# A third buffer for raw weights, a reordered opening, and constant products on TensorE ahead of the dense stage

## The chip, the cores and the metric

The kernel runs on one core of a Trainium2 chip. A core has five engines that run side by side and wait for each other by semaphores: TensorE (PE; its weight loads are listed as PEld), VectorE (DVE), ScalarE (ACT), GpSimd (POOL) and SyncE (SP), which here issues the DMA transfers from main memory. The metric is the device time of one execution in microseconds; the time before is 622.99 us, the median of three runs (621.7 to 623.39).

## The reference

Three stages follow each other.

```
# 1 attention-like scan, per batch and head (4 x 8), 768 tokens, head size 32, state 16
y = (C B^T * decay(i,j), causal) @ x  +  C @ state * decay_to_i
state = decay_full * state + sum_j decay_from_j * B_j x_j
x = y as 3072 tokens x 256
# 2 dense stage, w_a and w_b 256 x 1536, w_out 1536 x 256
x = ((x @ w_a) * (x @ w_b)) @ w_out
# 3 routed stage, 8 experts: each token goes to the expert of its largest logit
e = argmax(x @ w_gate); out = p[e] * sigmoid(x @ w_output_gate)[e] * relu(x @ w1[e]) @ w2[e]
```

The weights w_a, w_b, w_out come as 64-bit floats.

## The kernel before

**Tiling.** The 3072 tokens are 24 chunks of 128 tokens (index t), six to a batch. The dense stage takes them in nine blocks, BLK = 2, 2, 2, 2, 4, 4, 4, 2, 2 chunks. Its 1536 inner columns are 12 slices (index f) of 128. A unit (m, f) is block m times slice f: `unit_a` and `unit_b` make the two products on TensorE, VectorE multiplies them (L540), ACT and POOL split the result into two parts `gh` and `gl` (L427, L428), and `unit_o` adds it into the output. Each product is three TensorE passes over high and low parts (`mm3`, L513), so a unit of 256 tokens is 18 matmuls.

**Weights.** `load_w(f)` (L434) brings one slice of the three weights into a buffer `raw` by three DMAs (L439 twice, L442). `split_w(f)` turns the 64-bit numbers into a high part `whi` and a low part `wlo` in six pieces: ACT makes `u` (L464), VectorE does `low3` (L468), `sign` (L472) and `join` (L476), ACT rounds to `whi` (L480), VectorE subtracts to `wlo` (L483). The pool `stg` holds the raw slices; it has two buffers (L72), so the load of slice f+2 waits until slice f has been read.

**A chunk of the scan.** `tr` transposes B and C on TensorE (L339) and ACT copies them out, scaled (`cd`, L343, and `BT`, L345). `cb` multiplies them (L365, `pcb`), and VectorE multiplies the result with the decay mask `lm` that POOL has made (L303): this is the mask product (L369, `mt`). `ys` makes the outputs and the new state's part on TensorE (L386 to L396, `py`); ACT and VectorE split the output into `xh` (L402) and `xl` (L403), and VectorE updates the state (L407, L411). `prep` makes the scaled B and C for two chunks on POOL (`cp`, `Cq`, `Bq`, L295) and the masks.

**Decays.** `decays(r)` works out the decay factors of half r of the batches on VectorE, some 30 small instructions (L213 to L252), transposes them (`ex`, L207) and reduces the chunk totals (`tot` on POOL, L257, `tots` on VectorE, L264).

**What sets the order.** Each engine works its instructions off in the order in which they stand. From L993 the first steps are written out by hand (the opening). Behind them the units run in phases; after each product `tick` takes some steps of the scan from a list, two background steps (`bgstep`) and, by a rate, some pieces of the weight split from the list `dq` (`dstep`). Within that a scheduler places instructions of the four compute engines. A unit that needs a slice that is not yet split first takes the pieces that are missing. In the first three phases run blocks 0 to 3 with slices 0 to 5 while chunks 2 to 8 of the scan are worked; later phases run the other slices and blocks.

Of the kernel before, what the change touches and what calls it, by code (L numbers as in the profile page):

```python
# [7 lines left out]
F32 = mybir.dt.float32  # L8
# [10 lines left out]
def kernel(  # L19
# [52 lines left out]
    stg = ctx.enter_context(tc.tile_pool(name="stg", bufs=2))  # L72
# [93 lines left out]
    def load_bc(u):  # L166

        v = wk.tile([P, 2, G, H, N], F32, tag="BCin", name="BCin")
        for j, src in ((1, B), (0, C)):
            for i in range(G):  # L170
                b, c = divmod(u * G + i, NCH)
                nc.sync.dma_start(
                    out=v[:, j, i], in_=src[b, :, c * P:(c + 1) * P, :].rearrange("h p n -> p h n"))
        BCin[u] = v
# [12 lines left out]
    rfs = cst.tile([NR, 2, P], F32, name="rfs")  # L187
# [5 lines left out]
    def decays(r):  # L193
# [5 lines left out]
        ar = araw[:, r, :]  # L199
        rf, rs = rfs[:, 0], rfs[:, 1]  # L200
        a0, T, A, Eb, t2, t3 = (small(n) for n in ("a0", "T", "A", "Eb", "t2", "t3"))
        bc = lambda t, n=SUB: t.unsqueeze(2).to_broadcast([NR, n, SP_])
# [37 lines left out]

        def ends():

            q = st["q"]
            V.tensor_copy(out=A, in_=a0)
            for i in range(SUB - 1):
                V.tensor_scalar(out=A[:, i + 1:], in0=A[:, i + 1:], scalar1=T[:, i:i + 1], scalar2=None, op0=ALU.mult)
            for i in range(1, SUB):
                V.tensor_scalar(out=Eb[:, 0:i], in0=Eb[:, 0:i], scalar1=T[:, i:i + 1], scalar2=None, op0=ALU.mult)
            V.tensor_tensor(out=sub(q[:, 1]), in0=sub(q[:, 0]), in1=bc(A), op=ALU.mult)
            V.tensor_tensor(out=sub(q[:, 2]), in0=sub(rs), in1=bc(Eb), op=ALU.mult)  # L250
            V.tensor_tensor(out=t3[:, 0:1], in0=T[:, 0:1], in1=Eb[:, 0:1], op=ALU.mult)
            V.tensor_copy(out=q[:, 3], in_=t3[:, 0:1].to_broadcast([NR, P]))  # L252
# [14 lines left out]
        return dict(new=new, factors=factors, pairs=pairs, ends=ends, tot=tot, tots=tots,  # L267
# [55 lines left out]
    def attn_stages(t):  # L323
# [51 lines left out]
        def ys(alt=False):  # L375
# [23 lines left out]
            if m not in xT:  # L399
# [3 lines left out]
            nc.vector.tensor_tensor(out=lo[:, :, i0:i0 + P], in0=py,  # L403
                                    in1=hi[:, :, i0:i0 + P].bitcast(F32), op=ALU.subtract)
            if c < NCH - 1:
# [4 lines left out]
                if c > 0:  # L410
                    nc.vector.scalar_tensor_tensor(out=Sst, in0=Sst, scalar=dec[:, t:t + 1], in1=tm,  # L411
                                                   op0=ALU.mult, op1=ALU.add)

# [31 lines left out]
    def split_w(f):  # L445
# [7 lines left out]
        def wide_pieces(s):  # L453
# [1058 lines left out]
```

## Time and profile before

| | us |
|---|---|
| median of three runs | 622.99 |
| the profiled execution | 621.96 |
| its span, first to last instruction | 620.3 |
| TensorE busy | 569.3 (92%) |
| VectorE busy | 325.5 (52%) |
| ScalarE busy | 243.8 (39%) |
| GpSimd busy | 248.4 (40%) |

The profile is of one execution. Busy time is the sum of an engine's instructions without its waits. Of the 51 us in which TensorE is idle, 23.9 lie in the first 50 us and 8.3 in the next 50; from 100 to 400 us it is idle for 1.2 us. The granted clock is that of TensorE; 1.00 stands for 2.4 GHz and 0.50 for 1.2 GHz. Until the record's first change, at 43.5 us, the row shows 1.00 whatever the clock was; matmuls of 256 columns start 0.21 us apart at 21 us and 0.12 us apart at 51 us, which is the ratio of the two levels.

### The profile page before, as it was taken

The numbers are of one execution on the slowest core, as the hardware profiler recorded it, in microseconds if no ns is written. First come the engines' busy times: TensorE is split into PE (matmuls) and PEld (weight loads), VectorE is DVE, ScalarE is ACT, GpSimd is POOL, SyncE is SP. The second block draws the span as 40 slices with busy tenths as digits, with TensorE's granted clock in tenths as the row PEclk, the third lists the DMA queues.
The fourth block names the chain that finished last, engine by engine and source line by source line (L and its number), as shares of the span: only waits on it lengthen the run. The fifth ranks groups of instructions, "written<-read, shape, count | busy, mean of one in ns | idle before, by whom it ended". The sixth has DMA issues, their size and how long they took to land. (4 is left out here: it accounts for less than half of the span.)

```text
span 620.3 us, 11180 instructions
## 1 busy us (share of the span) xinstructions
PE 569.3 (92%) x4188; PEld 496.4 (80%) x4188; DVE 325.5 (52%) x894; ACT 243.8 (39%) x533; POOL 248.4 (40%) x319
## 2 busy tenths in 40 slices
PE   4369987999999999999999999999899999999991
PEld 2247867999897777777777889899788999999991
DVE  6779986224744434344232334544857556847620
ACT  3335553344333332332342233353345435445530
POOL 5547664333634433434222322364334433333111
PEclk9998997999999999999999999999999999999996
DMA  8597450002213210211000001221528345245000
GB/s 154 133 143 173 125 131 1 1 1 35 45 29 52 26 28 1 35 42 12 1 1 18 19 0 38 70 87 28 167 74 275 109 143 173 83 138 183 24 22 20
DMA packets 104920, 44.09 MB, mean 71 GB/s; under 512 B 81982, under 2 KB 99592, under 8 KB 104864
## 3 DMA queue, kind: packets, MB, share of 16 engines
q1 hardware_dynamic: 102128, 36.24, 23.7%
q0 software_dynamic: 2736, 7.12, 3.7%
q8 instruction: 34, 0.56, 0.4%
q14 instruction: 22, 0.18, 0.1%
HBM read 36.85 MB, written 6.95 MB: 71 GB/s over the span
## 5 line engine op out<-in xcount | busy, mean ns | idle before, releaser
L513 PE MATMUL pb<-xh,whi 128*128 128x256 f32 (+1 forms) x216 | 73.2, 339 | 1.7 <-ACT as__4671 L530 0.9
L513 PE MATMUL pa<-xh,whi 128*128 128x256 f32 (+1 forms) x216 | 72.0, 333 | 0.5 <-ACT xh L402 0.5
L513 PE MATMUL px<-gh,whi 128*128 128x256 f32 (+1 forms) x216 | 70.9, 328 | 0.0
L513 PE MATMUL pa<-xl,whi 128*128 128x256 f32 (+1 forms) x216 | 69.8, 323 | 0.0
L513 PE MATMUL px<-gl,whi 128*128 128x256 f32 (+1 forms) x216 | 69.2, 321 | 0.6 <-POOL gl L428 0.6
L513 PE MATMUL pa<-xh,wlo 128*128 128x256 f32 (+1 forms) x216 | 69.5, 322 | 0.0
L513 PE MATMUL px<-gh,wlo 128*128 128x256 f32 (+1 forms) x216 | 69.3, 321 | 0.0
L513 PE MATMUL pb<-xl,whi 128*128 128x256 f32 (+1 forms) x216 | 69.2, 320 | 0.0
L513 PE MATMUL pb<-xh,wlo 128*128 128x256 f32 (+1 forms) x216 | 69.1, 320 | 0.0
L1101 ACT ACTIVATE hh<-ph 128x384 fp32r<-128x384 f32 (+3 forms) x64 | 34.0, 531 | 69.7 <-PE ph L513 57.1
L1102 DVE SCALAR_TENSOR_TENSOR hl<-ph,hh 128x384 fp32r<-128x384 f32 (+3 forms) x64 | 38.7, 605 | 39.3 <-ACT hh L1101 33.8
L303 POOL TENSOR_SCALAR_AFFINE_SELECT lm<-EX 128x256 f32<-128x256 f32 x96 | 48.5, 541 | 24.2 <-DVE mt L369 22.6
L1121 PE MATMUL py<-eh,hh 128*128 128x256 f32 x200 | 57.0, 285 | 0.4 <-DVE hl L1102 0.4
L1121 PE MATMUL py<-el,hh 128*128 128x256 f32 x200 | 56.2, 281 | 0.0
L1121 PE MATMUL py<-eh,hl 128*128 128x256 f32 x200 | 56.1, 280 | 0.0
L1137 POOL DMA_INDIRECT out_dram<-yo,si x28 | 29.8, 1064 | 54.5 <-ACT yo L1134 47.7
L646 POOL DMA_INDIRECT xg<-x2d,gi x28 | 29.8, 1063 | 52.8 <-ACT lgx L661 36.9
L513 PEld LDWEIGHTS pb<-xh,whi 128*128 128x128 f32 x216 | 41.2, 191 | 10.7 <-issue 4.4
L513 PEld LDWEIGHTS pa<-xh,whi 128*128 128x128 f32 x216 | 41.3, 191 | 7.8 <-issue 3.7
L513 PEld LDWEIGHTS px<-gh,whi 128*128 128x128 f32 x216 | 41.0, 190 | 5.3 <-issue 2.1
L513 PEld LDWEIGHTS pa<-xh,wlo 128*128 128x128 f32 x216 | 41.4, 192 | 3.6 <-issue 0.3
L513 PEld LDWEIGHTS pa<-xl,whi 128*128 128x128 f32 x216 | 41.4, 192 | 3.3 <-issue 0.4
(685 smaller groups left out, 1402.3 us busy)
## 6 DMA issues: line engine op xcount, KB each, us to landing
raw<-in_moe_w_dram SPq DMA_DIRECT2D x30, 512.0 KB, 3.5
x2d<-xr SPq DMA_DIRECT2D x12, 272.0 KB, 2.2
xin<-in_x_dram SPq DMA_DIRECT2D x24, 128.0 KB, 2.9
raw<-in_moe_w_a_dram SPq DMA_DIRECT2D x12, 256.0 KB
raw<-in_moe_w_b_dram SPq DMA_DIRECT2D x12, 256.0 KB, 3.6
raw<-in_moe_w_out_dram SPq DMA_DIRECT2D x12, 256.0 KB, 4.1
BCin<-in_B_dram SPq DMA_DIRECT2D x26, 64.0 KB, 3.2
BCin<-in_C_dram SPq DMA_DIRECT2D x26, 64.0 KB, 3.1
```

Of the source, the lines that this page charges most:

```text
L303: nc.gpsimd.affine_select(out=Lm[t][:, :, s * SP_:(s + 1) * SP_], in_=exq(4 + s, b, c0 + i, 1).to_broadcast([P, H, SP_]), pattern=[[0, H], ...
L513: nc.tensor.matmul(out=out_, lhsT=l_, rhs=r_, start=first and i == 0, stop=last and i == 2, skip_group_check=skip)
L646: nc.gpsimd.indirect_dma_start(out=xg[:, q, :], out_offset=None, in_=x2d[0:nr, :], in_offset=bass.IndirectOffsetOnAxis(ap=sel["gi", i][:, ...
L1101: nc.scalar.activation(out=hh, in_=ph, func=AF.Relu)
L1102: V.scalar_tensor_tensor(out=hl, in0=ph, scalar=0.0, in1=hh.bitcast(F32), op0=ALU.max, op1=ALU.subtract)
L1121: nc.tensor.matmul(out=po, lhsT=l_[:, s_], rhs=r_, start=(f == 0 and j == 0 and q % 2 == 0), stop=(f == NF2 - 1 and j == 2), skip_group_ch ...
L1137: ins = nc.gpsimd.indirect_dma_start(out=out, out_offset=bass.IndirectOffsetOnAxis(ap=si[0:n_], axis=0), in_=yo, in_offset=None, bounds_ch ...
```

## The change

The pool of raw slices gets a third buffer. The loads of the first chunks are issued one chunk at a time, x of chunk 1 and all of chunk 0 and 1's B and C ahead of any weights; slices 0, 1 and 2 are loaded in the opening; later loads are taken from the list `dq` (`more_w`). The split of slice 1 moves from the opening into `dq`; pieces of slice 0's second and third part move ahead of steps of the scan. Eight small steps of `decays(0)` go to POOL (`parts`). `decays(1)` is put in the list at chunk 9 instead of 7, and its pieces stand ahead of `prep` there. The state update goes ahead of `xl` (L403). The function `warm` puts 15 products of a constant with itself on TensorE; nothing reads them. The tiles `u` share the buffers of `xr` and `x2T` for slices under 6, and from slice 6 on have one buffer instead of two. `rfs` moves into a shared buffer.

```
-    stg = ctx.enter_context(tc.tile_pool(name="stg", bufs=2))
+    stg = ctx.enter_context(tc.tile_pool(name="stg", bufs=3))
...
+        def parts(g=None):
+            g = g or V
+            g.tensor_copy(out=A, in_=a0)
+            for i in range(SUB - 1):
+                g.tensor_scalar(out=A[:, i + 1:], in0=A[:, i + 1:], scalar1=T[:, i:i + 1], scalar2=None, op0=ALU.mult)
+            for i in range(1, SUB):
+                g.tensor_scalar(out=Eb[:, 0:i], in0=Eb[:, 0:i], scalar1=T[:, i:i + 1], scalar2=None, op0=ALU.mult)
+            g.tensor_tensor(out=all_, in0=T[:, 0:1], in1=Eb[:, 0:1], op=ALU.mult)
...
-                    tl["u"] = wk.tile([P, 3 * DM], U32, tag="w64v", name="u", bufs=2)
+                    tag = ("xr", "x2T")[f % 2] if f < NE else "w64v"
+                    tl["u"] = wk.tile([P, 3 * DM], U32, tag=tag, name="u", bufs=1)
...
         load_a(0)
-        load_bc(0)
+        load_bc(0, 0)
         consts_early()
         load_x(0)
+        load_bc(0, 1)
+        load_x(1)
         load_w(0)
-        load_x(1)
-        load_bc(1)
         load_w(1)
+        load_bc(1, 0)
         load_x(2)
+        load_bc(1, 1)
         load_x(3)
+        load_w(2)
         load_a(1)
...
-                if t == 7:
-                    d1 = decays(1)
-                    nop = lambda: None
-                    bg.extend([d1["new"], d1["factors"], d1["pairs"], d1["ends"], nop, nop, nop, nop,
-                               d1["ex"](0, 4), d1["ex"](4, 4), d1["tot"], d1["tots"]])
+                if t == 9:
+                    d1 = decays(1)
+                    bg.extend(d1[k_] for k_ in ("new", "factors", "pairs", "parts", "ends"))
...
+        def warm(n):
+            t_ = pp([P, P], name="warm")
+            for _ in range(n):
+                nc.tensor.matmul(out=t_, lhsT=ones, rhs=ones, start=True, stop=True)
...
         s0["tr"]()
+        warm(2)
+        dc["parts"](nc.gpsimd)
         dc["ex"](4, 2)()
...
         s1["tr"]()
+        warm(3)
...
         dc["tot"]()
+        wb[0]()
+        wb[1]()
+        wb[2]()
+        wb[3]()
         s1["cb"]()
+        warm(2)
         s0["ys"](True)
+        warm(3)
         wa[5]()
+        wb[4]()
+        wb[5]()
+        wo[0]()
         dc["tots"]()
-        wb[0]()
         s1["ys"]()
-        for f_ in wb[1:] + wo:
+        warm(3)
+        for f_ in wo[1:]:
             f_()
```

**Where instructions stand.** On SP, the load of slice 2 before (what is in square brackets is what the instruction waits for; DMAHW is an earlier DMA, the others are engines):

```order
L439 DMA raw<-in_moe_w_a_dram 128x2x256 [waits DMAHW6_49]
L439 DMA raw<-in_moe_w_b_dram 128x2x256 [waits DMAHW7_49]
L442 DMA raw<-in_moe_w_out_dram 128x512 [waits DMAHW0_49]
L179 DMA xin<-in_x_dram 128x8x32 [waits DMAHW1_49]
L179 DMA xin<-in_x_dram 128x8x32 [waits DMAHW2_49]
L191 DMA araw<-in_a_dram 96x128 [waits DMAHW3_49]
```
```order
L179 DMA xin<-in_x_dram 128x8x32 [waits DMAHW0_49]
L179 DMA xin<-in_x_dram 128x8x32 [waits DMAHW1_49]
L439 DMA raw<-in_moe_w_a_dram 128x2x256 [waits DMAHW2_49,DVE_49,Activation_49]
L439 DMA raw<-in_moe_w_b_dram 128x2x256 [waits DMAHW3_49]
L442 DMA raw<-in_moe_w_out_dram 128x512 [waits DMAHW4_49]
```

The first piece ends with the loads of slice 1, the second is that of slice 2. In the changed kernel slice 1 and slice 2 stand on SP as follows:

```order
L442 DMA raw<-in_moe_w_a_dram 128x2x256 [waits DMAHW2_49]
L442 DMA raw<-in_moe_w_b_dram 128x2x256 [waits DMAHW3_49]
L445 DMA raw<-in_moe_w_out_dram 128x512 [waits DMAHW4_49]
L172 DMA BCin<-in_B_dram 128x8x16 [waits DMAHW5_49]
L172 DMA BCin<-in_C_dram 128x8x16 [waits DMAHW6_49]
L178 DMA xin<-in_x_dram 128x8x32 [waits DMAHW7_49]
L172 DMA BCin<-in_B_dram 128x8x16 [waits DMAHW0_49]
L172 DMA BCin<-in_C_dram 128x8x16 [waits DMAHW1_49]
L178 DMA xin<-in_x_dram 128x8x32 [waits DMAHW2_49]
L442 DMA raw<-in_moe_w_a_dram 128x2x256 [waits DMAHW3_49]
L442 DMA raw<-in_moe_w_b_dram 128x2x256 [waits DMAHW4_49]
L445 DMA raw<-in_moe_w_out_dram 128x512 [waits DMAHW5_49]
```

The load of slice 2 no longer waits for VectorE and ACT, and stands ahead of the second half of `a` and of x of chunks 4 and 5.

On ACT, from the output of chunk 1 (`xh<-py`) to the copies `cd` and `BT` of chunk 2, before:

```order
L402 ACTIVATE xh<-py 128x2x128
L480 ACTIVATE whi<-t 128x256
L464 ACTIVATE u<-raw 128x256
L480 ACTIVATE whi<-t 128x256
L464 ACTIVATE u<-raw 128x768
L480 ACTIVATE whi<-t 128x768
L464 ACTIVATE u<-raw 128x768
L530 ACTIVATE as__362<-pa 128x256
L464 ACTIVATE u<-raw 128x768
L343 ACTIVATE cd<-ptr,head_81 128x128 x2
L345 ACTIVATE BT<-ptr 128x256
```

and in the changed kernel:

```order
L405 ACTIVATE xh<-py 128x2x128
L484 ACTIVATE whi<-t 128x256
L468 ACTIVATE u<-raw 128x768 x2
L534 ACTIVATE as__372<-pa 128x256
L346 ACTIVATE cd<-ptr,head_81 128x128 x2
L348 ACTIVATE BT<-ptr 128x256
L484 ACTIVATE whi<-t 128x768
```

Between them stood two pieces of slice 0, slice 1 whole and the `u` of slices 2 and 3; now one piece of slice 0 and the `u` of slices 1 and 2.

On VectorE, a part of `decays(1)` before, between the multiplications L540 of the units of the third phase's first half:

```order
L238 TENSOR_SCALAR q_1054<-rfs,t_981 96x32
L246 TENSOR_SCALAR A_978<-A_978,T_977 96x3
L540 TENSOR_TENSOR as__905<-pb,as__905 128x256
L246 TENSOR_SCALAR A_978<-A_978,T_977 96x2
L248 TENSOR_SCALAR Eb_979<-Eb_979,T_977 96x1
L246 TENSOR_SCALAR A_978<-A_978,T_977 96x1
L248 TENSOR_SCALAR Eb_979<-Eb_979,T_977 96x2
L249 TENSOR_TENSOR q_1054<-q_1054,A_978 96x128
L248 TENSOR_SCALAR Eb_979<-Eb_979,T_977 96x3
L476 SCALAR_TENSOR_TENSOR t<-u,t 128x768
```

and its first instructions in the changed kernel (`as__1136` there is the multiplication that is called `as__1170` before):

```order
L544 TENSOR_TENSOR as__1136<-pb,as__1136 128x256
L476 SCALAR_TENSOR_TENSOR t<-raw 128x768
L487 TENSOR_TENSOR wlo<-t,whi 128x768
L544 TENSOR_TENSOR as__1175<-pb,as__1175 128x256
L480 SCALAR_TENSOR_TENSOR t<-u,t 128x768
L588 COPY x2T<-px_878 128x256
L213 MEMSET q_1848 96x96
L213 MEMSET q_1848 96x64
L544 TENSOR_TENSOR as__1203<-pb,as__1203 128x256
L487 TENSOR_TENSOR wlo<-t,whi 128x768
L213 MEMSET q_1848 96x32
L214 MEMSET Eb_1822 96x4
```

All of `decays(1)` on VectorE has moved behind the multiplication `as__1136`; its `tots` follows later still, ahead of the state update of chunk 9.

## Rows read from the trace of the kernel before

**Rows 1.** Windows: length, then busy (count) of PE, PEld, DVE, ACT, POOL, clock, DMA share, GB/s

```profile
36.06:99.10 63.04, 52.76 (x465) 43.24 (x465) 53.76 (x138) 30.67 (x71) 42.14 (x54) 0.91 0.58 131
104.53:200.00 95.47, 94.83 (x872) 87.73 (x871) 39.78 (x120) 38.23 (x101) 40.24 (x64) 1.00 0.16 24
...
43.50:50.20 6.70, 6.67 (x48) 4.83 (x49) 3.74 (x10) 2.18 (x5) 4.34 (x7) 0.50 0.72 212
...
94.30:101.35 7.05, 5.16 (x22) 4.54 (x23) 5.94 (x13) 1.26 (x2) 3.47 (x6) 0.53 0.00 0
```

**Rows 2.** Timeline of TensorE: start, length, what, [idle before it <- what ended it]

```profile
17.64 0.80 PE L386 MATMUL py<-BT,Sst 64*128 64x128 f32 x4 [1.73 <-DVE Sst L407]
...
20.38 0.58 PE L513 MATMUL pa<-xh,whi 128*128 128x256 f32 x1 [0.50 <-ACT xh L402]
...
34.48 1.24 PE L365 MATMUL pcb<-cd,BT 32*128 32x256 f32 x8 [11.56 <-ACT BT L345]
...
87.74 0.82 PE L207 MATMUL pd<-ident,q 96*128 96x96 f32 x8
...
96.19 1.22 PE L365 MATMUL pcb<-cd,BT 32*128 32x256 f32 x4 [3.84 <-DVE stm L407]
```

**Rows 3.** Timeline of ACT between the first two outputs and chunk 2

```profile
19.94 0.38 ACT L402 ACTIVATE xh<-py 128x256 fp32r<-128x256 f32 x1 [3.25 <-PE py L396]
23.03 0.42 ACT L480 ACTIVATE whi<-t 128x256 fp32r<-128x256 f32 x1 [2.71 <-DVE t L476]
...
30.18 0.37 ACT L530 ACTIVATE as__362<-pa 128x256 f32<-128x256 f32 x1
32.72 0.91 ACT L464 ACTIVATE u<-raw 128x768 f32<-128x768 f32 x1 [2.17 <-DMA raw<-in_moe_w_out_dram]
33.55 0.60 ACT L343 ACTIVATE cd<-ptr,head 128x128 f32<-128x128 f32 x2
34.04 0.38 ACT L345 ACTIVATE BT<-ptr 128x256 f32<-128x256 f32 x1
```

**Rows 4.** Timeline of SP, issues of the raw slices and of x

```profile
4.08 0.58 SPq L179 DMA_DIRECT2D xin<-in_x_dram  x1
...
24.65 0.37 SPq L439 DMA_DIRECT2D raw<-in_moe_w_a_dram  x1
```

**Rows 5.** VectorE by line, 36.06 to 99.10: count | busy, mean ns | idle before

```profile
L369 DVE TENSOR_TENSOR mt<-pcb,lm 128x256 f32<-128x256 f32 (+1 forms) x21 | 9.6, 503 | 3.9 <-PE pcb L365 3.9
L483 DVE TENSOR_TENSOR wlo<-t,whi 128x768 fp32r<-128x768 f32 x8 | 8.7, 1091 | 0.1
L472 DVE SCALAR_TENSOR_TENSOR t<-raw 128x768 uint32<-128x768 uint32 x7 | 8.5, 1217 | 0.0
L476 DVE SCALAR_TENSOR_TENSOR t<-u,t 128x768 uint32<-128x768 uint32 x8 | 8.5, 1057 | 0.0
L468 DVE TENSOR_SCALAR raw<-raw 128x768 uint32<-128x768 uint32 x7 | 4.6, 651 | 0.0
```

**Rows 6.** Timeline of VectorE

```profile
2.75 0.22 DVE L218 TENSOR_SCALAR araw<-araw 96x128 f32<-96x128 f32 x1 [1.31 <-DMA araw<-in_a_dram]
...
9.18 0.45 DVE L252 COPY q<-t 96x128 f32<-96x128 f32 x1
...
36.06 1.35 DVE L369 TENSOR_TENSOR mt<-pcb,lm 128x256 f32<-128x256 f32 x3
...
94.13 0.32 DVE L264 TENSOR_REDUCE dec<-dtmp 128x12 f32<-128x96 f32 x1 [2.94 <-POOL dtmp L257]
...
99.10 0.42 DVE L540 TENSOR_TENSOR as__1170<-pb,as__1170 128x256 f32<-128x256 f32 x1 [0.96 <-PE pb L513]
...
104.53 0.42 DVE L540 TENSOR_TENSOR as__1237<-pb,as__1237 128x256 f32<-128x256 f32 x1 [0.49 <-PE pb L513]
...
106.65 0.42 DVE L540 TENSOR_TENSOR as__1269<-pb,as__1269 128x256 f32<-128x256 f32 x1 [0.73 <-PE pb L513]
```

**Rows 7.** Timeline of POOL in the opening

```profile
1.88 0.20 POOL L132 TENSOR_TENSOR headh<-headm 128x4 f32<-128x4 f32 x1
...
8.59 4.02 POOL L303 TENSOR_SCALAR_AFFINE_SELECT lm<-EX 128x256 f32<-128x256 f32 x8 [1.65 <-ACT EX L208]
```

More of the change, by code (lines that the diff above doesn't have):

```diff
@@ L164, with load_bc @@
     xin, BCin = {}, {}
-    def load_bc(u):
-        v = wk.tile([P, 2, G, H, N], F32, tag="BCin", name="BCin")
+    def load_bc(u, i):
+        if i == 0:
+            BCin[u] = wk.tile([P, 2, G, H, N], F32, tag="BCin", name="BCin")
+        b, c = divmod(u * G + i, NCH)
         for j, src in ((1, B), (0, C)):
[L170 to L174, printed above, removed]
+            nc.sync.dma_start(out=BCin[u][:, j, i],
+                              in_=src[b, :, c * P:(c + 1) * P, :].rearrange("h p n -> p h n"))
     def load_x(t):
@@ L186 @@
     seed = cst.tile([NR, P], F32, name="seed")
-    rfs = cst.tile([NR, 2, P], F32, name="rfs")
     def load_a(r):
@@ L265, in tots @@
                             in_=st["tmp"].rearrange("p b h c -> p b c h"), axis=AX.X, op=ALU.add)
-        return dict(new=new, factors=factors, pairs=pairs, ends=ends, tot=tot, tots=tots,
+        return dict(new=new, factors=factors, pairs=pairs, parts=parts, ends=ends, tot=tot, tots=tots,
                     ex=lambda k0, n: lambda: to_ex(k0, n))
@@ L906, with more_w @@
                                   in_=src[k * P:(k + 1) * P, :])
-        done = {"x": 4, "bc": 2}
+        done = {"x": 4, "bc": 2, "w": 3}
         bg = []
         RATE = [1.2, 0.6, 0.3, 0.4, 0.8]
-        dq = []
-        late_, first = [], []
-        for f in range(NF1 + 1):
+        def more_w():
+            if done["w"] < NF1:
+                load_w(done["w"])
+                done["w"] += 1
+        first = split_w(0)
+        dq = split_w(1) + [more_w]
+        late_ = []
+        for f in range(2, NF1 + 1):
             ps = split_w(f) if f < NF1 else []
-            if f < 2:
-                first.append(ps)
-                ps = []
             dq.extend(late_[:1] + ps[:1] + late_[1:])
-            late_ = ps[1:]
-            if f + 2 < NF1:
-                late_.append(lambda f=f: load_w(f + 2))
+            late_ = ps[1:] + [more_w]
         due = [0.0]
@@ L930, in dstep, with more_bc @@
                 due[0] -= 1
+        def more_bc():
+            for i in range(G):
+                load_bc(done["bc"], i)
+            done["bc"] += 1
         def ahead(t):
@@ L1033 @@
         ahead(1)
-        bg.append(lambda: (load_bc(2), done.update(bc=3)))
-        bgstep()
-        for f_ in w1_:
-            f_()
-        bgstep()
-        dstep(2)
+        bg.append(more_bc)
+        bgstep(2)
         tc.no_sync_barrier()
```

24 lines of the change are left out of this document (12 added, 12 removed).

## The prediction

> **What bounds the kernel now.** I read the windows first, then TensorE's waits in order of time, then what VectorE does while TensorE waits. From 104.53 to 200 us TensorE is busy for 94.83 of 95.47 us while VectorE is busy for 39.78 [rows 1]; the table of the profile shows the same up to 400 us. There the time is TensorE's work, and the change leaves that work and its order alone, but for eight small transposes. So what the change is worth is the time at which TensorE enters this full stretch.
>
> Ahead of it the reader is to see two large waits of TensorE. At 34.48 it has waited 11.56 us for the copy `BT` of chunk 2, at 96.19 it has waited 3.84 us for a state step of VectorE [rows 2]. The first wait is one of ACT's queue: `BT` (34.04) stands behind `u` of slice 3, which at 32.72 had itself waited 2.17 us for the last third of that slice [rows 3]. The raw loads had been held back: slice 2 was issued only at 24.65, when a buffer came free [rows 4]. The second wait is one of VectorE: `tots` of `decays(1)` waited 2.94 us for POOL's `dtmp` at 94.13 [rows 6], and the state step stands behind it.
>
> Between the two waits VectorE is the fuller engine. From its mask product of chunk 2 at 36.06 to the multiplication `as__1170` at 99.10 [rows 6] it is busy for 53.76 of 63.04 us, idle for 9.28 [rows 1]; TensorE's 52.76 us there [rows 1] hold stretches at half clock, as 43.50 to 50.20, where the granted clock is 0.50, that is 1.2 GHz [rows 1]. So I keep a ledger of VectorE over this stretch and ask where the multiplication that stood at 99.10 comes to stand.
>
> **The opening, up to chunk 1's output.** A load of x now stands ahead of the second C load on SP; such an issue took 0.58 us [rows 4], and all that follows from `cp` comes 0.6 later. The 15 products of `warm` have no row. Nearest is L386: two products of 128 columns in 0.80 us [rows 2], 0.4 each. Eleven of them stand where TensorE waits anyway (the wait of 1.73 us for the state [rows 2] is one such place); two ahead of the transposes `pd` and two ahead of chunk 0's outputs stand on the path to chunk 1's output: 1.6 us, less what other waits hide; I take 0.9. Bounds: none on the path, 0, and all on it, 6.0. The eight steps of `parts` go to POOL: a POOL step of four numbers took 0.20 us [rows 7], so 1.6 us, in POOL's wait of 1.65 us ahead of its masks [rows 7]: nothing. If the cover is gone, the masks come 1.6 later.
>
> The Trainium skill, page GPSIMD Engine Reference, section "Engine selection", advises against this: elementwise work with two inputs is about twice as slow on GpSimd. No row sets the same step on both engines against each other; by the rule the eight steps would take twice as long, 3.2 us, and the masks and the sum come 1.6 us later.
>
> So chunk 1's `xh` ends at 20.32 + 0.6 + 0.9 = 21.8 instead of 20.32 (19.94 + 0.38 [rows 3]).
>
> **The first wait.** Behind `xh` of chunk 1 ACT now has one piece's `whi`, two `u` and one copy `as` before `cd` and `BT`. From the end of `xh` to the end of the next `whi` took 3.13 us (20.32 to 23.45 [rows 3]), with the same VectorE steps between them, and I keep that; two `u` of 0.91, `as` 0.37, `cd` and `BT` together 0.87 (33.55 to 34.42 [rows 3]). 21.8 + 3.13 + 1.82 + 0.37 + 0.87 = 28.0: `pcb` of chunk 2 starts at 28.0 instead of 34.48. Slice 2 must have landed by 25; it is loaded without a wait for a buffer, right behind the first chunks. `pcb` takes 1.24 us [rows 2] and its first bank can be used a little before its end: the mask product starts at 29.0 instead of 36.06, **-7.1 us**.
>
> **The ledger of VectorE from there.** Less had been done by then. In the changed order `wlo` of slices 1 and 2, `join` of 2 and `low3` and `sign` of 3 stand behind the mask product, ahead of it before; and at the end `low3` of slice 11 is in and was not. At the means of this stretch [rows 5]: 2 x 1.09 + 1.06 + 0.65 + 1.22 + 0.65 = **+5.8 us**.
>
> `decays(1)` leaves the stretch. The same instructions for the first half ran in the opening from 2.75 to 9.63 without a real gap [rows 6], 6.9 us; two of them (0.4) were done before 36.06 already, the total at 94.13 of 0.32 goes with them less what instructions overlap: **-6.5 us**. They come back behind `as__1136` and near chunk 9, where VectorE is idle for more than half of the time [rows 1]; a wait for `dtmp` there is covered by that. The eight transposes `pd`, 0.82 us [rows 2], move into the stretch in which TensorE is full: **+0.8 us**.
>
> Idle time: of 9.28 us the 2.94 for `dtmp` goes. The 3.9 for `pcb` [rows 5] came from late operands of chunks 3 and 4; POOL can now make them ahead, since their B and C stand on SP ahead of slice 3 now and behind it before, and most of that should go. New small waits will come, since the same chain of mask product, output, state step and next `pcb` is still there. I take 4, so **-5.3 us**; bounds 1 and 9.3.
>
> Sum for the ledger: 53.76 + 5.8 - 6.5 + 4 = 57.1 us from 29.0: the multiplication that stood at 99.10 stands at 86.1, 13.0 earlier. TensorE can follow: its 52.76 us held 6.7 at half clock from 43.50 and more around it, so at full clock it needs under 50.
>
> **The clock behind the second wait.** From 94.30 to 101.35 the granted clock is 0.53 [rows 1], after TensorE had been idle for 3.84 us [rows 2]. From 99.10 to 104.53 took 5.43 us, in which two units were done; two units at full clock are 2 x 2.12 (104.53 to 106.65 [rows 6]). With `dtmp` gone from ahead of the state step that wait should be near 1 us and the clock stay up: **-1.2 us**. If it falls as before: 0.
>
> **Single edits at nothing.** The third buffer and the order of `dq` put off further pieces of the split; they fall where VectorE has room. The state update ahead of `xl` is 0.4 us for TensorE, in the noise of the 4 us above.
>
> **The sum.** -13.0 - 1.2 + 0.8 = -13.4 us. The profiled execution goes from 621.96 to 608.6 (span 620.3 to 606.9). The median is 1.0 above the profiled execution, so I predict 609.5 us for the median.
>
> **Rivals.** (A) VectorE takes the stall over: TensorE no longer waits at 34 us, but the mask products wait for it as long as before. For it speaks that VectorE was held by waits on the chain of the scan, not by loads, for 3.9 us. Idle 9.3 instead of 4 gives 614.8, and all of `warm` on the path gives up to 619. (B) The clock rises before the dense stage. Before, the first output enters at 20.38 [rows 2] and at 43.50 the clock is still found at half [rows 1]. If `warm` keeps TensorE busy enough for 2.4 GHz at 22 us and it stays there, its steps between the first mask products halve, about 3 us in the chain, and with idle of 2 the time is 604.5. Against it: TensorE still waits some 3 us for `BT` of chunk 2, and a wait of 3.84 us cost the clock at 94.30. The Trainium skill, page TensorE: Matmul & The Clock Gate, Part 1, says that half rate is the default and that activity lifts it, which is this case's reading; by it `warm` would act, and (B) would be the time; no row here shows these products. (C) The change doesn't do what it says: slices 0 to 2 and the small rows of B and C share the DMA engines, slice 2 or chunk 2's B lands at 28 to 30 us instead of 25, and the first wait shrinks by 3 us less: 612.5, inside my range. (D) Slower: from slice 6 on `u` has one buffer, so ACT waits in `u` of a slice for `join` of the one before, with the copies `as` and `gh` queued behind it, and TensorE behind these. If each of the five waits cost the whole split of a slice on VectorE (0.65 + 1.22 + 1.06 + 1.09 = 4.0 us [rows 5]), 20 us, the time would be 622.99 - 13.4 + 20 = 629.6; it decides from 2.7 us each. Against it: the instruction behind `u` on ACT is `whi` of the slice before, which needs that same `join`, so only `u`'s own 0.9 us is added, beside other work.
>
> **How the numbers follow.** Chances: the forecast (606 to 614) 0.62, (A) with a late opening (614 to 621) 0.17, (B) 0.12, (C) alone beyond the forecast's range 0.03, (D) or another loss 0.06. The range takes (B)'s 604.5 less 1.5 for an idle time of 1 us, and (A)'s 614.8 plus 2.2 for `warm`: 603 to 617, which leaves out about 0.15 to 0.2. A difference under 0.3% (1.9 us) can't be told from none in this kernel. Faster by more than that 0.92, within it 0.03, slower 0.05.
>
> **What would show it.** `pcb` of chunk 2 on TensorE at 26 to 30 us, with `BT` on ACT right behind `u` of slice 2 and no DMA wait: the first wait. No `decays(1)` on VectorE ahead of its multiplication `as__1136`, which starts at 83 to 90: the ledger. No wait over 2 us of TensorE ahead of the `pcb` of chunk 8 and a granted clock of 1.00 there: the clock. From there to the end the same length as before within 2 us. The prediction is wrong if VectorE's idle time in the ledger grows past 9 us, if TensorE's full stretch holds a new wait (at chunks 9 and 10, where `decays(1)` now is), or if the end comes later by another path than the entry into the full stretch.

## The result, and the profile after

The changed kernel takes 619.02 us (median of ten runs, 614.32 to 620.42) against 623.19 us for the kernel before beside it: a ratio of 0.990, with an interval of 0.987 to 0.993. In a second set of runs it takes 613.24 against 621.41, 0.986 (0.983 to 0.989). So it is faster by 4 to 8 us, not by 13; the first set lies outside the range given, the second inside it. Ratios, here and below, leave out four slow executions (643 us of e3, 711 of e5, 617.6 of e15 and 1107 of the kernel before). Two things separate the forecast from the first result: TensorE enters the full stretch 6 us later than forecast, and 5 us of what was won are lost again at 447 us, in a place at which the prediction did not look.

The profiled execution takes 619.64 us, its span is 617.9 instead of 620.3. First the opening on POOL and ACT, then VectorE from the opening to the ledger's end (start, length, what, [idle before it <- what ended it]):

```profile
7.64 0.64 POOL L298 TENSOR_TENSOR cp<-BCin,EX 128x256 f32<-128x256 f32 x1 [5.28 <-DMA BCin<-in_C_dram]
8.22 0.18 POOL L244 COPY A<-a 96x4 f32<-96x4 f32 x1
8.51 1.08 POOL L246 TENSOR_SCALAR A<-A,T 96x3 f32<-96x3 f32 x3
9.56 1.21 POOL L248 TENSOR_SCALAR Eb<-Eb,T 96x1 f32<-96x1 f32 x3
10.85 0.29 POOL L249 TENSOR_TENSOR all<-T,Eb 96x1 f32<-96x1 f32 x1
11.10 3.22 POOL L306 TENSOR_SCALAR_AFFINE_SELECT lm<-EX 128x256 f32<-128x256 f32 x8
```

```profile
24.41 0.38 ACT L405 ACTIVATE xh<-py 128x256 fp32r<-128x256 f32 x1 [1.80 <-PE py L399]
```

```profile
11.17 3.22 DVE L255 COPY q<-all 96x128 f32<-96x128 f32 x1
...
28.28 1.71 DVE L472 TENSOR_SCALAR raw<-raw 128x768 uint32<-128x768 uint32 x2
29.91 2.35 DVE L476 SCALAR_TENSOR_TENSOR t<-raw 128x768 uint32<-128x768 uint32 x2
32.18 1.04 DVE L480 SCALAR_TENSOR_TENSOR t<-u,t 128x768 uint32<-128x768 uint32 x1
33.14 1.34 DVE L372 TENSOR_TENSOR mt<-pcb,lm 128x512 f32<-128x512 f32 x3
...
92.52 0.41 DVE L544 TENSOR_TENSOR as__1136<-pb,as__1136 128x256 f32<-128x256 f32 x1
...
96.52 0.35 DVE L544 TENSOR_TENSOR as__1203<-pb,as__1203 128x256 f32<-128x256 f32 x1
```

In the kernel before, `cp` and the first steps of `parts` (on VectorE there) stood as follows:

```profile
6.29 0.64 POOL L295 TENSOR_TENSOR cp<-BCin,EX 128x256 f32<-128x256 f32 x1 [3.94 <-DMA BCin<-in_C_dram]
```

```profile
7.08 0.73 DVE L246 TENSOR_SCALAR A<-A,T 96x3 f32<-96x3 f32 x3
```

`cp` comes 1.35 us later than before. Behind it `parts` runs on POOL from 8.22 to 11.14, so the masks start at 11.10 instead of 8.59 [rows 7], and beside them the copy `q` on VectorE takes 3.22 us; before it took 0.45 [rows 6]. The output of chunk 1 (`xh`) ends at 24.79 instead of 20.32 [rows 3]. On TensorE `pcb` of chunk 2 follows at 30.29; the wait of 11.56 us [rows 2] is one of 3.22 now. But five split instructions of VectorE (28.28 to 33.14) stand ahead of its mask product, which starts at 33.14 (36.06 before). The columns of the second view are length, busy time (count) of PE, PEld, DVE, ACT and POOL, granted clock, DMA share, GB/s:

```profile
30.29 0.71 PE L368 MATMUL pcb<-cd,BT 32*128 32x256 f32 x8 [3.22 <-ACT BT L348]
```

```profile
33.14:92.52 59.38, 53.76 (x459) 43.20 (x460) 53.83 (x113) 31.39 (x71) 32.68 (x42) 0.85 0.56 134
38.41:51.00 12.59, 12.59 (x65) 8.31 (x66) 7.85 (x15) 3.69 (x8) 5.92 (x10) 0.50 0.71 194
94.30:101.35 7.05, 7.05 (x63) 7.05 (x62) 6.81 (x22) 3.36 (x8) 6.78 (x11) 1.00 0.00 0
447.00:457.23 10.23, 10.23 (x50) 10.23 (x50) 2.51 (x11) 0.69 (x2) 0.00 (x0) 0.52 0.00 0
```

The products of the dense stage are the same in both kernels, so their lead can be read product by product. At the second multiplication by `pb` (51.39 before, 51.13 after) 0.3 us of lead are left of what the first wait gave; at the fourteenth it is 1.2; at the fifteenth, the ledger's end, 6.6 (99.10 [rows 6] to 92.52); at the seventeenth 8.0 (104.53 [rows 6] to 96.52); from 200 to 430 us 7.4. Then comes `phB`, the first product of the last routed block, which waits for the copy `xB`; before, then after:

```profile
453.64 3.79 PE L1417 MATMUL phB<-xB,raw 128*128 128x64 f32 x32 [1.34 <-ACT xB L1410]
```

```profile
446.91 6.72 PE L1447 MATMUL phB<-xB,raw 128*128 128x64 f32 x32 [2.06 <-ACT xB L1440]
```

Behind a wait of 2.06 us TensorE works at 1.2 GHz: 50 instructions take 10.23 us (window above). The same 50 took 5.81 before:

```profile
453.64:459.45 5.81, 5.81 (x50) 5.81 (x51) 2.61 (x11) 0.73 (x3) 0.00 (x0) 1.00 0.19 61
```

The loss is 4.4 us of clock and 0.7 of longer wait. It fits the spread of the ten runs, of which one was profiled: eight have a mean granted clock of 0.964 to 0.970 and take 617.0 to 620.4, two have 0.976 and 0.977 and take 615.5 and 614.3.

### The profile page after: what moved, and what is told of

Read it like the earlier page. It is cut to its first block, busy times and chain, and to the rows that moved or that the text cites. A ratio compares the mean times of both kernels' runs of the same rounds, so it can differ in the third digit from the quotient of the medians.

```text
span 617.9 us, 11231 instructions
## 1 busy us (share of the span) xinstructions
PE 576.9 (93%) x4218; PEld 503.7 (82%) x4218; DVE 329.9 (53%) x886; ACT 243.1 (39%) x533; POOL 250.1 (40%) x327
## 3 DMA queue, kind: packets, MB, share of 16 engines
HBM read 36.59 MB, written 6.95 MB: 70 GB/s over the span
## 4 chain that ended last, share of the span: by engine, by line
PE 75%; DVE 12%; issue 5%; DMA 2%; POOL 2%; ACT 1%; SPq 1%; another core or an unknown queue 0%; POOLq 0%; DVEq 0%; ACTq 0%
PE px L517 14%; PE pb L517 13%; PE pa L517 13%; PE py L1151 11%; PE ph L517 11%; PE ptx L723 2%; PE pcb L368 2%; PE py L393 2%; DVE t L476 1%; DVE t L480 1%; DVE mt L372 1%; PE py L389 1%; DVE raw L472 1%; PE phB L1447 1%; PE ptg L1113 1%
## 5 line engine op out<-in xcount | busy, mean ns | idle before, releaser
L306 POOL TENSOR_SCALAR_AFFINE_SELECT lm<-EX 128x256 f32<-128x256 f32 x96 | 45.7, 511 | 9.2 <-DVE mt L372 9.1
L517 PEld LDWEIGHTS px<-gh,wlo 128*128 128x128 f32 x216 | 40.8, 189 | 4.6 <-issue 1.3
```

Of the source, the lines that this page charges most:

```text
L306: nc.gpsimd.affine_select(out=Lm[t][:, :, s * SP_:(s + 1) * SP_], in_=exq(4 + s, b, c0 + i, 1).to_broadcast([P, H, SP_]), pattern=[[0, H], ...
L517: nc.tensor.matmul(out=out_, lhsT=l_, rhs=r_, start=first and i == 0, stop=last and i == 2, skip_group_check=skip)
```

## The experiments

Each label's ratio is to the kernel before in the same set of runs (e1 to e4 are one set, e5 to e8 the second, e9 to e12 and e13 to e15 two more). The last two columns are of the profiled execution alone: its time, and the start of its fifteenth multiplication by `pb` (99.10 before). It is the fastest of its runs in e5, e10, e11, e14 and e15 and the slowest in e8 and e13, so these columns show where time lies, and the medians decide.

| run | us | ratio (95%) | profiled, us | 15th, us |
|---|---|---|---|---|
| e1 fill ahead of phB | 614.44 | 0.990 (0.988-0.993) | 613.92 | 92.51 |
| e2 no constant products | 613.35 | 0.989 (0.986-0.991) | 613.41 | 92.65 |
| e3 parts on VectorE | 611.52 | 0.985 (0.981-0.988) | 611.52 | 91.40 |
| e4 decays behind chunk 7 | 615.30 | 0.992 (0.990-0.995) | 615.20 | 96.73 |
| e5 changed kernel again | 613.24 | 0.986 (0.983-0.989) | 612.17 | 91.48 |
| e6 before + decays moved | 616.97 | 0.992 (0.989-0.995) | 618.36 | 97.47 |
| e7 e3 + products at chunk 2 | 608.58 | 0.979 (0.976-0.981) | 608.75 | 88.39 |
| e8 two raw buffers | 613.04 | 0.986 (0.983-0.989) | 614.59 | 94.41 |
| e9 late xB | 620.51 | 0.997 (0.996-0.999) | 620.85 | 92.66 |
| e10 late xB, filled | 617.26 | 0.994 (0.992-0.996) | 614.04 | 91.01 |
| e11 first loads as before | 611.53 | 0.984 (0.982-0.986) | 608.71 | 88.16 |
| e12 e3 + six products | 611.37 | 0.984 (0.982-0.986) | 613.43 | 91.65 |
| e13 slice 1 in the opening | 618.10 | 0.991 (0.989-0.994) | 619.68 | 95.84 |
| e14 the parts that helped | 608.33 | 0.977 (0.975-0.980) | 606.37 | 85.00 |
| e15 e6 + order of pieces | 612.42 | 0.985 (0.982-0.988) | 607.40 | 85.13 |

In the executions that kept the clock at `phB`, the span ends 516.8 to 521.3 us behind the fifteenth multiplication; in the three that lost it, wholly or in part (the first profile, e9, e13), 522.2 to 526.5. So the entry into the full stretch and `phB` set the time between them.

The expectations of e1 to e4 start from the 619.0 us of the first set, which holds the loss at `phB`. None of the four profiles has that loss, so their times come out lower than these texts say; they are compared here with each other.

### The loss at phB

e1, six products ahead of `phB`:

```
+            warm(6)
             ph = pp([P, NF2, CAPB], name="phB")
```

> The changed kernel with six more unread products on TensorE right ahead of the first products phB of the last block, where it waits 2.06 us for the copy xB. Theory: the changed kernel enters the full stretch about 7.4 us earlier and keeps that lead up to 440 us; some 5 us of it are lost at 447 to 459 us, because this wait takes the granted clock from 1.00 to 0.50, and phB and the products behind it run at half speed. Then with the wait filled the clock stays at 1.00 there, phB takes 3.8 us instead of 6.7, and the time is 619.0 - 5 = 614, within 1 us. Rival: the 5 us are lost to the wait itself or to the chain of gathered rows behind it, and the clock has no part in it; then the filled wait changes nothing: 618 to 620, or up to 1 us more if the six products push phB back.

e5, no edit:

> The changed kernel itself once more, beside the kernels of this call. In its first profile it led the kernel before by 7.4 us up to 440 us and lost 5 of them where phB waited 2.06 us for xB and the clock fell to 0.50 (phB 6.72 us instead of 3.79). Theory: this loss is no fixed part of the change, since three kernels that differ from it only in the opening and the scan waited 0.2 us there and kept the clock; then in a run in which that wait stays short the time is 6 to 7 us under the kernel before, a ratio of 0.989 to 0.991, and phB takes 3.8 us. Rival: the changed kernel always loses the clock there: phB 6.7 us again and a ratio of 0.996 to 0.998.

In the runs behind the first set `xB` came sooner: e5 waits 0.17 us, its `phB` takes 3.79 us, and its ratio is 0.986, somewhat better than the 0.989 to 0.991 of the theory. So the loss is no fixed part of the change. It also means that e1 had next to nothing to fill: 614.44 is the time that its theory gave, by luck, and tells nothing on the clock. To force the wait, e9 makes the copy nine times, and e10 adds e1's products:

```
-            nc.scalar.activation(out=sel["xB"], in_=pt, func=AF.Copy)
+            for _ in range(9):
+                nc.scalar.activation(out=sel["xB"], in_=pt, func=AF.Copy)
```

> The changed kernel with the copy xB on ScalarE done nine times over instead of once, so that TensorE waits some 2 us longer ahead of phB (0.2 us in the last profile of the changed kernel, 613.2 us). Theory: the wait itself costs 2 us, and because it takes the granted clock to 0.50 for the next 9 to 12 us it costs 4 to 5 more: phB 6.7 us instead of 3.8, 619 to 620.5 us, a ratio of 0.996 to 0.999 to the kernel before; this is what the first profile of the changed kernel lost. Rival: the wait alone counts, phB stays at 3.8 us, 615 to 616 (a ratio of 0.989 to 0.991).

> The same late copy xB, with six unread products on TensorE in the wait. Theory: TensorE reaches phB as late as without them, but at the full clock: phB 3.7 to 3.8 us and 615 to 616 us, 4 to 5 us under the kernel with the late copy alone. Rival: what was lost there was not the clock, and both take the same time within 1 us.

TensorE in e9, and the windows of the 51 instructions from `phB` on, in e9 and in e5:

```profile
448.12 6.57 PE L1448 MATMUL phB<-xB,raw 128*128 128x64 f32 x32 [2.65 <-ACT xB L1441]
```

```profile
448.12:458.50 10.38, 10.38 (x51) 10.38 (x52) 1.66 (x10) 0.74 (x3) 0.00 (x0) 0.53 0.00 0
```

```profile
444.19:450.00 5.81, 5.81 (x51) 5.81 (x52) 2.61 (x11) 0.73 (x3) 0.00 (x0) 1.00 0.08 24
```

The wait is 2.5 us longer than in e5, the time 7.3: the rest is the clock (10.38 us for 5.81), as the theory said. With the wait filled in part (e10) 3.3 us come back, where the theory had 4 to 5:

```profile
443.28 1.50 PE L1013 MATMUL warm<-ones 128*128 128x128 f32 x12
446.08 3.79 PE L1449 MATMUL phB<-xB,raw 128*128 128x64 f32 x32 [1.30 <-ACT xB L1441]
```

This execution kept the clock and took 614.04 us. The other six took 615.7 to 620.5 at a mean clock of 0.969 to 0.974, so in some of them it seems to have fallen all the same, behind the 1.3 us that stay unfilled. Waits of about that length went both ways here: behind 1.17 to 1.34 us ahead of `phB` the clock held in four profiled executions (the kernel before, e10, e14, e15), behind 1.21 us it fell in part in one (e13).

### The second half of the decays

e4 puts it back behind chunk 7; e6 moves it behind chunk 9 in the kernel before:

```
-                if t == 9:
-                    d1 = decays(1)
-                    bg.extend(d1[k_] for k_ in ("new", "factors", "pairs", "parts", "ends"))
...
+                if t == 7:
+                    d1 = decays(1)
```

> The changed kernel with the second half of the decays put back where it was in the kernel before, behind chunk 7 with four empty steps, and not behind chunk 9. Theory: of the lead of 7.4 us with which the changed kernel enters the full stretch only about 1 is there at 88 us, at the fourteenth multiplication by pb, and 5.4 come at the next, where the kernel before had the second half of the decays on VectorE and the wait for dtmp behind it. Put back, they take these 5 to 6 us again: 624 to 625. Rival: the other load order, the third buffer and the products gave the lead, and the decays only fill room: 618 to 620.5.

> The kernel before with one part of the change alone: the second half of the decays stands behind chunk 9 and no longer behind chunk 7; loads, buffers and products as before. Theory: this part is most of the gain. The multiplication by pb that stood at 99.10 comes 5 to 6 us earlier (93 to 94), the clock is 1.00 at 94 to 101, and the time is 5 to 6 us under the kernel before. Rival: the work only moves, and is as much in the way in the full stretch of TensorE as ahead of it; then 0 to 2 us under the kernel before.

The part is real, its size was put too high. e6 gains 4.4 us (a ratio of 0.992). Its fifteenth multiplication stands at 97.47, not at 93 to 94: the clock is 1.00 from 94 to 101 as expected, but with a wait of 1.9 us ahead of a `pcb` it had already fallen, to 0.50 from 86.4 to 93.2. e4 is 5.2 us under the kernel before where I expected 1 to 2 above it, and only 2 us above e2 in the same set. Its fifteenth multiplication is 4 to 5 us later than in the changed kernel, and some 2 us of that come back behind it. In e4 VectorE waits 1.45 us for `dtmp`, not 2.94 [rows 6].

### Third buffer, loads, products, parts

```
e8   -    stg = ctx.enter_context(tc.tile_pool(name="stg", bufs=3))
     +    stg = ctx.enter_context(tc.tile_pool(name="stg", bufs=2))
e11  load_bc(0,0) load_bc(0,1) load_x(0) load_w(0) load_x(1)
     load_bc(1,0) load_bc(1,1) load_w(1) load_x(2) load_x(3) load_w(2)
e2   warm: the products left out
e3   -        dc["parts"](nc.gpsimd)
     +        dc["parts"]()
```

> The changed kernel with two buffers for the raw weights, as before, so that slice 2 waits for the first buffer. Theory: the first wait hardly matters. With two buffers pcb of chunk 2 comes 3 to 5 us later than 30, but VectorE's work sets the entry into the full stretch, so the multiplication that stood at 92.5 moves by less than 1.5 us and the time by less than 1.5. Rival, the term of the prediction: the entry moves with pcb of chunk 2, and the time rises by 4 to 7 us.

> The changed kernel with its first loads in the order of the kernel before (both small rows of B and C of chunks 0 and 1 first, x of chunk 1 behind slice 0, slice 1 behind B and C of chunks 2 and 3); everything else, the order of every compute engine too, as in the changed kernel. Theory: about half of the gain of 8 us is not the decays (put alone into the kernel before they gave 4.4, 616.97 against 621.41) nor the third buffer nor the products, so it must come from the other order of loads and of the pieces of the split; if the loads are it, this kernel loses 3 to 4 us of it, 616 to 617. Rival: the pieces are it; the first loads only shift the opening, cp comes at 6.3 instead of 7.7, and since what is won there up to the second multiplication is gone at the fifth, the time stays within 1 us of the changed kernel's 613.2 (a ratio of 0.985 to 0.988).

> The changed kernel without the fifteen unread products. Theory: they cost little, since nearly all stand in waits, and what they bring (full clock from 20.6 to about 31 us) is lost at the wait for BT of chunk 2; the mask product of chunk 2 moves by under 1 us from 33.1, and the time stays at 617.5 to 620. Rival 1, the term of the prediction: those on the path to chunk 1's output made the opening late by 0.9 to 6 us; without them the mask product of chunk 2 comes at 28 to 32 and the time is 613 to 618. Rival 2: the full clock in the opening saves about 3 us in the chain; without it the time is 622.

> The changed kernel with the eight small steps of parts on VectorE instead of GpSimd. Theory: on GpSimd they took 2.9 us and pushed its eight masks from about 8.6 to 11.1, and beside the masks the copy of q on VectorE took 3.22 us instead of 0.45; with them on VectorE the masks start at 8 to 9, the copy takes about 0.5, and the mask product of chunk 1 comes 2 to 3 us earlier than 21.45. How much of it reaches the end: if the opening sets the entry into the full stretch, the mask product of chunk 2 comes at 30 to 31 instead of 33.1 and the time is 616 to 617. Rival: VectorE's work up to the last chunks of the scan sets the entry (it is busy for over 95% from 60 to 90 us), the copy only stalls in the place of a wait, and the time stays at 618 to 620.

Of the four only `parts` on VectorE brings a gain, and a small one.

- With two buffers (e8, first line below) `pcb` of chunk 2 waits 6.43 us and its mask product starts at 34.52. The time is that of e5 beside it (613.04, 613.24), although the fifteenth multiplication of the profiled execution is 2.9 us later than in e5, more than the 1.5 of the theory. The edit also changes what the scheduler puts where on all four engines, so e8 tests the buffer and that order together.
- The loads in the old order (e11) leave all orders as they are and are no slower (0.984), against the theory.
- The products of the opening are worth nothing either way: e2 takes 613.35, its fifteenth multiplication stands at 92.65, in e1 at 92.51.
- `parts` on VectorE (e3, second view below) takes the stall of the copy away (0.22 us) and brings the mask product of chunk 2 from 32.42 (e1) to 30.44. In e1, e2 and e3 the clock comes back at the same 51 us. The fifth multiplication stands at 59.39, 59.44 and 58.33, the fifteenth at 92.51, 92.65 and 91.40, and e3 takes 611.52 us against 613.35 in e2. So of the 2 us some 1.2 reach the entry, and the rival, by which nothing does, was right for the other part only. (e5 stands where e3 does, at 58.31 and 91.48; there the clock came back at 44.4 us, see the next section.)

```profile
33.13 1.24 PE L368 MATMUL pcb<-cd,BT 32*128 32x256 f32 x8 [6.43 <-ACT BT L348]
```

```profile
8.71 0.22 DVE L255 COPY q<-all 96x128 f32<-96x128 f32 x1
...
30.44 1.34 DVE L372 TENSOR_TENSOR mt<-pcb,lm 128x512 f32<-128x512 f32 x3
```

### The clock from 31 to 51 us

e12 has `parts` on VectorE and six products ahead of `pcb` of chunk 2, e7 ten there and two ahead of chunk 2's outputs:

```
+            if f is not None and k in ("cb", "ys") and t == 2:
+                def f(f=f, n=10 if k == "cb" else 2):
+                    warm(n)
+                    f()
```

> The changed kernel with parts on VectorE, and with ten more unread products where TensorE waits 3.3 us for BT of chunk 2 and two ahead of the outputs of chunk 2. To be read against the kernel with parts on VectorE alone, where TensorE runs at the full clock from 17 to 27 us, falls to 0.50 behind this wait and stays there to 51, with TensorE busy without a gap from 36. Theory: half the clock at 27 to 51 us eats the gain of the first wait; with the wait filled the clock stays at 1.00, the second multiplication by pb comes at 43 to 46 instead of 48.5, and what VectorE, which is full from 55 to 90, lets through of it is 1 to 3 us at the end. Rival: VectorE's work alone sets the entry; then the second multiplication comes earlier but the fifteenth stays at 91.4 within 0.5, and so does the time. Second rival: the clock falls at the next gap all the same, and nothing moves.

> The changed kernel with parts on VectorE and six unread products ahead of pcb of chunk 2, where TensorE waits 3.3 us for BT. Ten there and two further on gave 608.6, but they also changed the order in which the instructions of the scan stand on VectorE, ScalarE and GpSimd; six leave these orders as they are with parts on VectorE alone (611.5, a ratio of 0.9845). Theory: most of those 3 us came from the order, not the clock, since two executions of the changed kernel itself in which the clock rose at 44.5 and at 51 us were 3.1 us apart at the second multiplication and 1.0 at the fifth and all later ones. So with the same order: if the clock holds from 27 us on, the second multiplication comes at 43 to 46 and the time is 610 to 611.5 (a ratio of 0.981 to 0.985); if it falls all the same, nothing moves. Rival: the clock is what counted; then 608 to 609 (0.977 to 0.980).

e7 is 12.8 us under the kernel before, but it settles nothing on the clock: the wait that it fills comes back as one of 3.36 us for the mask product, the clock falls there, and the added products change what the scheduler puts where on VectorE, ACT and POOL. In e12, with the orders unchanged, 1.91 us of the wait remain, the clock falls and nothing moves (611.37). The windows of e7 and e12:

```profile
30.00:35.00 5.00, 1.64 (x9) 1.00 (x7) 5.00 (x8) 2.68 (x6) 4.30 (x8) 0.70 0.31 110
35.00:45.00 10.00, 10.00 (x79) 6.91 (x77) 7.15 (x13) 3.32 (x8) 7.26 (x10) 0.50 0.84 199
```

```profile
30.00:35.00 5.00, 3.72 (x36) 2.57 (x34) 5.00 (x8) 2.16 (x5) 4.55 (x9) 0.50 0.36 101
35.00:45.00 10.00, 9.05 (x56) 5.20 (x50) 6.67 (x14) 3.90 (x8) 6.76 (x10) 0.50 0.65 142
```

The nearest reading is from one program: up to `phB` the first profile, e1, e9, e5 and e10 are executions of the same instructions. Their windows from 31 to 51 us, in this order:

```profile
31.00:51.00 20.00, 17.76 (x105) 11.90 (x104) 14.79 (x26) 7.25 (x15) 12.33 (x20) 0.50 0.60 150
```

```profile
31.00:51.00 20.00, 17.88 (x106) 12.01 (x106) 14.55 (x27) 7.24 (x15) 11.20 (x19) 0.50 0.59 141
```

```profile
31.00:51.00 20.00, 18.29 (x108) 12.43 (x108) 14.32 (x27) 7.25 (x15) 12.37 (x20) 0.50 0.61 149
```

```profile
31.00:51.00 20.00, 18.60 (x135) 12.98 (x135) 16.69 (x30) 8.40 (x18) 11.31 (x16) 0.66 0.59 142
```

```profile
31.00:51.00 20.00, 18.03 (x115) 12.99 (x116) 16.14 (x28) 8.17 (x18) 13.00 (x22) 0.59 0.63 158
```

The second multiplication stands at 51.13, 50.41 and 50.23 in the three at half clock, at 48.03 in e5 and 48.87 in e10; the fifteenth at 92.52, 92.51 and 92.66 against 91.48 and 91.01. The first one, at 34.40, 33.69, 33.51, 33.51 and 34.05, does not decide this. So the half clock there is worth 1.0 to 1.7 us at the entry, as far as five executions tell.

### The order of the pieces

e13 is the changed kernel with slice 1 back in the opening; e15 is e6 with the pieces as in the changed kernel, and with the later loads taken from the list `dq` as there:

```
e13  -        dq = split_w(1) + [more_w]
     +        w1_ = split_w(1); dq = [more_w]
     ...
     -        bgstep(2)
     +        bgstep()
     +        for f_ in w1_:
     +            f_()
     +        bgstep()
     +        dstep(2)
e15  in e6: the reverse of e13, the order of wb and wo of the change, more_w in dq
```

> The changed kernel with the pieces of slice 1 back at the end of the hand-ordered opening, all ahead of the mask product of chunk 2, as in the kernel before. Theory: the place of the pieces is what is left of the gain; with slice 1 whole ahead of chunk 2, its mask product comes 1 to 3 us later, and the time is 615 to 617 (a ratio of 0.989 to 0.993). Rival: VectorE has to do these pieces before the entry into the full stretch wherever they stand; the multiplication that stood at 91.5 to 92.5 stays there within 1 us and the time stays at 612 to 614 (0.984 to 0.988).

> The kernel before with two parts of the change: the second half of the decays behind chunk 9, and the pieces of the split in the order of the changed kernel (four of the second piece of slice 0 ahead of chunk 1's pcb, slice 1 no longer in the opening); two buffers, loads in the order of before, no products, parts on VectorE. Theory: these two parts are the whole gain: 611 to 614 (a ratio of 0.983 to 0.988). Rival: the rest hangs on the earlier load of slice 2 and the order of loads behind it; then 616 to 617, as with the decays alone (0.992).

e15 went as the theory said, e13 in part. In e13 the mask product of chunk 2 stands at 36.59, 3.4 to 4.3 us later than in the changed kernel (1 to 3 expected), the fifteenth multiplication at 95.84, and the ratio is 0.991. But `phB` waited 1.2 us there, lost part of the clock (4.85 us), and from its start to the end 169.4 us passed, 166.3 in e5. So e13 shows the later entry, by 3 to 4 us, in its trace; its time holds some 3 us of the loss at `phB` too. The kernel before with the edits of e15 alone reaches 0.985, which is the whole gain of the changed kernel (0.986 in e5). Pieces and later loads were not tried apart in it. In e15, which keeps two buffers, `pcb` of chunk 2 starts at 25.36 and its mask product at 26.70. These rows are of an execution 5 us under the median, whose clock was 1.00 from 30 to 45 us:

```profile
25.36 1.24 PE L365 MATMUL pcb<-cd,BT 32*128 32x256 f32 x8 [2.40 <-ACT BT L345]
```

```profile
30.00:45.00 15.00, 11.87 (x114) 8.30 (x114) 14.75 (x41) 8.14 (x19) 14.42 (x19) 1.00 0.95 210
```

```profile
26.70 1.35 DVE L369 TENSOR_TENSOR mt<-pcb,lm 128x512 f32<-128x512 f32 x3 [0.21 <-PE pcb L365]
...
85.13 0.41 DVE L540 TENSOR_TENSOR as__1114<-pb,as__1114 128x256 f32<-128x256 f32 x1
```

### The parts that helped

e14 is e7 with e11's loads.

> The parts that helped, together: the changed kernel with parts on VectorE, the first loads in the order of the kernel before, and twelve unread products ahead of chunk 2, which with parts on VectorE alone gave 608.6 (a ratio of 0.9785). Theory: the older load order brought 1 to 2 us where all else was as in the changed kernel (0.984 against 0.986), and cp and the masks come 0.7 us earlier; 606 to 608 (0.974 to 0.977). Rival: what is won in the opening is gone at the fifth multiplication, as it was with parts on VectorE; 608 to 609.

608.33 us and 0.977 beat both kernels; against e7 (0.979) there is no difference that the intervals show, so the rival was right on the time, though the fifteenth multiplication stands 3.4 us earlier in this profile, which is of the fastest of five runs.

## Why the prediction was wrong

Three steps failed: the opening's cost on POOL, the start of chunk 2's mask product, and the length behind the entry, which was taken as unchanged.

**The opening.** `xh` of chunk 1 ended at 24.8, not 21.8. The step that failed is "in POOL's wait of 1.65 us ahead of its masks: nothing": the eight steps took 2.9 us, the second half of them alone 1.5, and held two more things up, VectorE for `A` and `Eb` and the copy beside the masks. `cp` ahead of them came 1.35 us later, not 0.6; the 0.9 for the products on the path was 0.1 (the same `xh` ends at 24.11 without them in e2, at 24.24 in e1). The rule quoted from the Trainium skill (page GPSIMD Engine Reference, section "Engine selection") is for two inputs, and the prediction put it on all eight steps. Only the last of them has two tensors as inputs (`all`: 0.29 us on POOL, 0.15 on VectorE in e3, near the rule); the three `L246` steps took 1.08 us on POOL and 0.73 on VectorE, a factor of 1.5, and all eight 2.9 and 2.0 (e3). The bounds held neither the waits nor the copy.

**The first wait.** `pcb` at 30.3 instead of 28.0 follows from that. The further step failed by itself: "its first bank can be used a little before its end: the mask product starts at 29.0". I took the mask product to be next on VectorE; 28.28 to 33.14 went to `low3` and `sign` of slices 1 and 2 and `join` of slice 1, which the order that came out put ahead of it. Why it did is not shown: in e8, where slice 2 lands later, pieces of slice 2 stand ahead of it as well. So the term was -2.9, not -7.1; of the 4.1 us that are missing 2.3 are the opening's and 1.8 this step's.

**The ledger** held otherwise: 53.83 us busy where I had 53.1, idle 5.55 where I had 4, 59.4 in all for 57.1. Its end at 92.52 instead of 86.1 is 4.1 from the start and 2.3 from the length. Its term for the moved decays, -6.5, is worth 4.4 us in the kernel before (e6) and 2 in the changed one (e4). "TensorE can follow" was wrong in this stretch: from 38.41 to 51.00 it was busy all the time at half clock, and the lead at the second multiplication was 0.3.

**The clock behind the second wait** was right: -1.4 (6.6 to 8.0) for -1.2, no wait over 1.02 us and a clock of 1.00. The way back in the full stretch was +0.6 (8.0 to 7.4) for +0.8; that the transposes are the cause is not shown.

**"Single edits at nothing"** had the sizes the wrong way round. The third buffer, on which the first wait's -7.1 rested, is worth nothing in e8's median. The order of `dq`, which I put at nothing, is with the moved decays the whole gain (e15).

**The end.** "From there to the end the same length as before within 2 us" failed in the first set: 5 us at `phB`. Of the 11 us between the forecast span of 606.9 and 617.9, 6.4 are the ledger's end and 5 this; the clock's better term takes a little back. e9 shows the mechanism. Why `xB` was late in the first profile is open: ScalarE started the instruction two places ahead of it after 2.23 us of idle time for which the record names no engine of this core, in e5 after 0.67.

The prediction's own list of what would prove it wrong has this last case: "if the end comes later by another path than the entry into the full stretch".

Rival (A) names the band in which the first set fell (614 to 621), but for the most part by luck. A late opening with VectorE in the stall's place is what the trace shows; but VectorE's idle time was 5.55 us, not (A)'s 9.3, the products did not make the opening late, and without the loss at `phB`, which (A) does not have, the time is the second set's 613.24, inside the forecast's 606 to 614. That nearness is no success either, since the largest term of the forecast, the -7.1 of the first wait, came to -2.9. Rival (B)'s early rise of the clock came (1.00 from 20.7 to 30.9 us), and was lost at the 3.22 us wait that its own text names. (C) and (D) did not show: ACT's `u` of slices 1 and 2 waited for no DMA, and the lead stays at 7.4 us from 200 to 430. Two sums of the prediction are slightly off, without weight for the outcome: 622.99 less 13.4 is 609.6, and (B) with an idle time of 1 us instead of 2 is 1.0 under 604.5, not 1.5.

Not settled: how much of e7's and e14's further gain is the clock and how much the changed order, and which of e15's edits besides the decays carries its part.

## What to carry to other kernels

Where one engine is full up to the point that sets the end, ask which of its work must stand ahead of that point, and move that; an operand that arrives earlier gains nothing past the work that stands ahead of its user. Price a wait of TensorE at the wait and the half clock behind it, in every place where the change moves it, also far behind the edits. A hand-made edit ahead of a scheduler's stretch is judged with the order that comes out, not with the edit. Where two executions of one program differ in the clock, compare variants at the same clock: e3's 1.2 us show only so.

## What was not expected of the hardware

A copy of 96 x 128 numbers on VectorE took 3.22 us from 11.17 on, exactly beside eight masks of GpSimd that had begun 0.07 us earlier, and 0.22 where it ran ahead of them (e3). It did so in all ten profiled executions with `parts` on GpSimd. In the kernel before the same copy ran beside the masks too, and took 0.45 us [rows 6, rows 7]; in e6 and e15 it took 0.51 and 0.45. The Trainium skill, page SBUF — State Buffer, section "Who interferes with whom", says that the two engines share a pair of ports as an exclusive lock, that a copy on VectorE can run in a mode that takes this pair, and that then whoever issues first has it for the whole instruction and the other is blocked. The trace of the changed kernel agrees, but there the copy was blocked over eight instructions, not one. No run shows the copy's mode, and why it was let in between the masks in the kernel before stays open.

One program found its full clock again at 44.4 us in one execution (e5) and at 51.4 in another (the first profile); the page TensorE: Matmul & The Clock Gate, Part 1, also of the Trainium skill, says that the ramp varies between runs of one kernel, as here.
